# A fused AFNO / GEGLU kernel: the gate/up contraction recut into pairs of 192 columns, the weight chain reordered

## The chip, the core and the metric

The kernel runs on one core of a Trainium2 chip. The metric is device time in microseconds of one execution; the time before is the median of three runs. TensorE multiplies, VectorE and ScalarE read its results out of PSUM, GpSimd takes a part of the elementwise work, SyncE issues nearly all transfers.

## The reference

One sequence of 8192 tokens with 448 features is normalised per token; two branches read it. The first is a spectral one: a Fourier transform over the tokens, a two-layer complex MLP in four blocks of 112 with ReLU and soft threshold, and the inverse transform. The second is a GEGLU feed-forward with 1792 hidden features. The output joins them.

```python
xn = layernorm(x)                                     # [8192, 448]
s  = irfft(softshrink(mlp2(relu(mlp1(rfft(xn))))))    # along the 8192 tokens
g  = silu((gelu(xn @ w_gate) * (xn @ w_up)) @ w_down) # 448 -> 1792 -> 448
out = x + s * g
```

## The kernel before

All products are made from fp16 halves: a value is split into hi and lo, and hi·hi + hi·lo + lo·hi are summed in PSUM, three matmuls for each tile of 128 contraction rows. TensorE's stream is led by the feed-forward; all else is put between its matmuls.

The feed-forward goes over the 14 tiles of 128 hidden features in two passes (`PF`): pass 0 with 8 tiles, whose partial result goes to memory (`prt`), pass 1 with 6. Each pass goes over 16 chunks of 512 tokens. Chunks 0 and 1 of pass 0 are multiplied plainly (`plain()`); all others use a Winograd form with seven products in place of eight: the token pairs and the 448 contraction columns are halved, the latter into K1 = 256 and K2 = 192. A *unit* (`unit()`) is two hidden tiles of one chunk: its steps a1 to a7 call `product(k)` for the seven classes, for each of the two tiles. The operand combinations of the tokens are made by `factors()` in the first phase, written to memory (`xts`), and read back transposed, XA / 128 = 16 tiles of them as `xta` and 9 as `xtb`. The combinations of the weights are made by `gu_comb()`. A class whose two row tiles are full takes six matmuls for one hidden tile; one whose second tile holds 64 hi and 64 lo rows takes five:

```python
PROD = {1: (0, 4), 5: (4, 8), 6: (8, 10), 7: (12, 12), 2: (3, 6), 4: (6, 14), 3: (0, 2)}
if k in (1, 5, 6, 7):
    seq = [(s, v + j, xb + 2 * d + j) for j in range(2) for s, d in ((0, 0), (0, 1), (1, 0))]
else:
    seq = [(0, v, xb), (0, v, xb + 2), (1, v, xb), (0, v + 1, xb + 1), (1, v + 1, xb + 1)]
```

The order of steps in a unit of `chunk()` is: product 5, product 6, product 4 of the unit before, product 2, product 3, product 1 of the next unit, product 7. ScalarE copies product 5 out (`copy5`), and VectorE adds the bank of products 1 and 6 to it (`sum5`); products 3 and 7 wait for that sum.

The down product of a chunk follows its units. It is plain at first (`down()`: 8 tiles x 4 token tiles x 3 = 96 matmuls of 448 columns) and takes a seven-product form (`down2()`: 7 x 4 x 2 x 3 = 168 matmuls of 224 columns and one of 64) from the first chunk at whose start `state` has "products", that is, once `factor0()` has written the combined down weights; that form also needs sums of the hidden values (`sums()`) and, in the middle of the next chunk's first unit, its own tail.

The spectral branch has three phases around it. Phase 1 (`chunk1()`) normalises the tokens of a chunk, makes the factors and the first Fourier stage (`stage1()`, three matmuls for each token tile); phase 2 (`group()`, 64 of them) does the second stage and the MLP, with `zero()` for frequency 0; phase 3 (`tiles3()`) the last stage and the output. The weight chain (`weights()`) runs beside phase 1: `gu_split()` and `gu_comb()` of the 8 near tiles, `factor0()`, the 6 far tiles in pairs (`far_block()`), the far down weights (`down_weights(1)`), the MLP weights (`prep_mlp()`). Staging tiles come from rings: `WS` for gate/up weights (4 buffers in the prologue, then 1), `WD`, `CB`, `WO`.

The order of all instructions is fixed when the kernel is built: generators are run by a planner (`Pace`) that keeps a model clock for each engine and starts work at times set by constants (`STEPS`, `T1`, `DT`, `END1` to `END3`). `calm()` and `lull()` put an instruction off until the planner sees its engine free. Every engine then runs its own list in order, and waits on semaphores.

Of the kernel before, what the change touches and what calls it, by code (L numbers as in the profile page):

```python
# [36 lines left out]
XA, XW = 4 * 2 * K1, 4 * 2 * K1 + 3 * 2 * K2  # L37
SL = 11
# [3 lines left out]
STEPS = ((0, 2.75, 0.05, 0.97), (100, 2.5, 0.2, 1.03), (175, 3, 0.15, 1.0), (250, 2.75, 0.1, 1), (325, 2.5, 0.05, 1.01), (400, 2.75, 0.05, 1.04), (475, 3.0, 0.05, 1), (550, 3.5, 0.05, 1.01), (700, 2.75, 0.05, 1.02), (775, 2.0, 0.1, 0.985), (850, 2.25, 0.05, 0.97), (925, 2.75, 0.05, 1.04), (1150, 2.75, 0.05, 0.985), (1450, 2.5, 0.05, 1.01), (1525, 2.75, 0.15, 0.99))  # L42
# [342 lines left out]
def fft_constants():  # L385
# [45 lines left out]
    def triple(v, scale):  # L431
        hi, lo = _split(v * scale)
        return np.stack([hi, lo, (hi.astype(np.float64) * 2.0 ** -11).astype(np.float16)], axis=1)

    small = np.concatenate([
# [9 lines left out]
        "c_small": np.ascontiguousarray(small),  # L445
    }
# [3 lines left out]
def lay_out(a):  # L450

    up, gate = (np.asarray(a[k]).reshape(D, NF, 128) for k in ("B_w_up", "B_w_gate"))
    gu = np.zeros((NF, 128, SL, 128), np.float32)
    for s, w in ((0, up), (4, gate)):
        gu[:, :, s:s + 3] = w[:384].reshape(3, 128, NF, 128).transpose(2, 1, 0, 3)
    for s, w, r in ((3, up, 384), (7, gate, 384), (8, gate, 128), (10, up, 128)):
        gu[:, :64, s] = gu[:, 64:, s] = w[r:r + 64].transpose(1, 0, 2)
    gu[:, :64, 9] = gu[:, :64, 3]
# [5 lines left out]
        "in_gu": gu.reshape(NF, 128, SL * 128),  # L464
# [9 lines left out]
def afno_geglu_kernel(ctx, tc, x, gu, wd, mlp, b1, b2, c_m, c_mt, c_small, out):  # L474
# [44 lines left out]
    ident = cp.tile([128, 128], F16, name="ident")  # L519

# [4 lines left out]
    fm = cp.tile([128, 2, 2, NBK], F32, name="fm")  # L525
    fx = cp.tile([128, 2, 2 * NBK], F32, name="fx")
# [27 lines left out]
    def largest(dst, src, floor):  # L554
# [11 lines left out]
        V.tensor_scalar(dst, b[:, 128:128 + w], floor, None, op0=ALU.max)  # L566
# [20 lines left out]
    p1 = r1.enter_context(tc.tile_pool(name="p1", bufs=1, side="right"))  # L587
    X4 = ring(p1, [128, CH, D], F32, "x4", 2)
# [4 lines left out]
    SX = ring(p1, [128, 4 * 480], F16, "sx", 2)  # L593
    MX = ring(p1, [8, 1], BF16, "mxr", 2)
    identb = p1.tile([128, 128], BF16, name="identb")
# [3 lines left out]
    WS = ring(wp, [128, SL * 128], F32, "wst", 4)  # L599
# [197 lines left out]
    def far_block(b):  # L797
# [9 lines left out]
        for i in range(2):  # L807
# [5 lines left out]
            if i == 0:  # L813
                WS.put(t)
# [1867 lines left out]
```

## Time and profile before

| | |
|---|---|
| median of three runs | 1755.29 us (1753.55 to 1756.8) |
| profiled execution | 1756.02 us, span 1754.1 us |
| granted TensorE clock, mean | 0.997 |
| TensorE busy | 1724.0 us, 16218 matmuls |
| VectorE / ScalarE / GpSimd busy | 1432.7 / 1123.8 / 739.2 us |
| traffic | 304.16 MB, mean 173 GB/s |

A matmul's busy time overlaps that of its neighbours, so the time of one is read from the distance of two starts. A tile's name stands for all its buffers; nearly every instruction has the same line, since one helper issues them, and so groups are told apart by their tiles: `wt` are gate/up weights, `dw` down weights, `h` and `left` the hidden values, `xs` the token halves, `bx`, `by`, `bd` PSUM banks.

### The profile page before, as it was taken

How to read it: one execution, taken by the hardware profiler on the slowest of the kernel's cores; microseconds unless marked ns; L12 is line 12 of the kernel's file. 1: busy time of each engine (PE TensorE's matmuls, PEld its weight loads, DVE VectorE, ACT ScalarE, POOL GpSimd, SP SyncE). 2: the span in 40 equal slices, each digit the busy share in tenths (PEclk: the TensorE clock that was granted, in tenths of full speed). 3: DMA queues.
4: the chain of work that ended last, by engine and by line, in shares of the span. 5: the costliest groups of instructions: out<-in, count | busy, mean ns of one | idle time of the engine just before them, and what ended most of it. 6: DMA issues, size and time to landing. Idle time of an engine off the chain costs nothing.

```text
span 1754.1 us, 41652 instructions
## 1 busy us (share of the span) xinstructions
PE 1724.0 (98%) x16218; PEld 1489.0 (85%) x16218; DVE 1432.7 (82%) x2558; ACT 1123.8 (64%) x2244; POOL 739.2 (42%) x910
## 2 busy tenths in 40 slices
PE   8999999999999999999999999999999999999998
PEld 4447678899888899999989899898999889888887
DVE  7868677887988978777888787899888887788888
ACT  6557666666667666566887777777777775433334
POOL 2124333655666755253533545455434442122221
PEclk9999999999999999999999999999999999999999
DMA  6374788665666664323456755654456545999986
GB/s 224 104 214 151 202 229 220 192 192 167 166 202 208 197 169 126 73 63 93 107 164 189 177 122 130 153 129 103 122 137 144 129 103 132 300 293 330 312 249 223
DMA packets 402006, 304.16 MB, mean 173 GB/s; under 512 B 272688, under 2 KB 372912, under 8 KB 401808
## 3 DMA queue, kind: packets, MB, share of 16 engines
q1 hardware_dynamic: 401664, 301.46, 61.2%
q8 instruction: 127, 2.08, 0.5%
q14 instruction: 71, 0.58, 0.1%
q10 hardware_dynamic: 144, 0.03, 0.0%
HBM read 131.44 MB, written 106.15 MB: 135 GB/s over the span
## 4 chain that ended last, share of the span: by engine, by line
PE 82%; DVE 9%; ACT 3%; issue 2%; DMA 2%; SPq 1%; POOL 1%; DVEq 0%; ACTq 0%
PE bd L234 33%; PE bx L234 27%; PE by L234 22%; DVE h L234 2%; DVE wt L234 1%; ACT h L234 1%; SPq L234 1%; DVE u L234 1%; DVE left L234 1%; DVE va L234 1%; DVE v L234 0%; DMA vt<-va 0%; DMA wsp<-wo 0%; DVE by L234 0%; ACT wt L234 0%
## 5 line engine op out<-in xcount | busy, mean ns | idle before, releaser
L234 PEld LDWEIGHTS <-wt 128*128 128x128 f16 x9350 | 905.8, 98 | 168.8 <-issue 12.4
L234 PE MATMUL bx<-xta,wt 128*128 128x256 f16 (+1 forms) x2979 | 371.6, 275 | 3.2 <-DVE by L234 2.6
L234 PEld LDWEIGHTS <-h 128*128 128x128 f16 x2716 | 258.8, 98 | 36.4 <-DVE h L234 3.9
L234 PE MATMUL by<-xtb,wt 128*128 128x256 f16 x2080 | 256.4, 273 | 3.4 <-DVE by L234 3.4
L234 PE MATMUL bd<-dw,h 128*128 128x224 f16 (+1 forms) x1266 | 171.0, 280 | 1.2 <-DVE h L234 1.1
L234 POOL TENSOR_TENSOR wt<-wt 128x256 f32<-128x256 f32 x97 | 76.6, 790 | 200.1 <-DVE wt L234 182.4
L234 PE MATMUL by<-xta,wt 128*128 128x256 f16 (+1 forms) x1059 | 141.8, 281 | 3.2 <-ACT wt L234 3.1
L234 PE MATMUL bx<-xtb,wt 128*128 128x256 f16 x1040 | 131.6, 274 | 0.5 <-DVE v L234 0.4
L234 ACT ACTIVATE u<-by,fc 128x512 f32<-128x512 f32 (+1 forms) x118 | 73.6, 636 | 49.7 <-PE by L234 46.7
L234 PE MATMUL bx<-left,wt 128*128 128x256 f16 x864 | 105.1, 273 | 0.0
L234 DVE TENSOR_TENSOR by<-bx,u 128x512 f32<-128x512 f32 x104 | 72.1, 693 | 38.8 <-PE bx L234 32.4
L234 PE MATMUL bd<-dw,wt 128*128 128x224 f16 (+1 forms) x816 | 98.7, 264 | 2.2 <-DVE left L234 1.8
L234 ACT COPY u<-by 128x512 f32<-128x512 f32 x104 | 60.8, 585 | 61.5 <-PE by L234 61.2
L234 ACT CAST h<-wt 128x512 f16<-128x512 f32 (+1 forms) x128 | 68.5, 536 | 34.9 <-DVE wt L234 27.9
L234 PE MATMUL bd<-wt,h 128*128 128x224 f16 x693 | 84.3, 259 | 1.2 <-DVE h L234 1.1
L234 PEld LDWEIGHTS <-left 128*128 128x128 f16 x864 | 81.9, 98 | 3.1 <-issue 0.8
L234 DVE TENSOR_TENSOR v<-bx,u 128x512 f32<-128x512 f32 x104 | 71.2, 685 | 13.6 <-PE bx L234 12.6
L234 ACT COPY by<-bx 128x512 f32<-128x512 f32 x104 | 60.0, 577 | 34.8 <-PE bx L234 34.6
L234 PE MATMUL bd<-w2t,wn 113*128 113x112 f16 (+1 forms) x1152 | 77.3, 212 | 0.9 <-DVE bd L234 0.7
L234 DVE SCALAR_TENSOR_TENSOR left<-bd,ms,left 128x448 f32<-128x448 f32 x96 | 64.3, 677 | 16.9 <-PE bd L234 15.9
L234 ACT ACTIVATE th<-bd,ms 128x448 f32<-128x448 f32 x62 | 38.6, 634 | 59.6 <-PE bd L234 54.4
L234 POOL TENSOR_TENSOR t<-h 112x256 f32<-112x256 f32 (+1 forms) x40 | 35.1, 877 | 96.3 <-ACT h L234 73.9
(294 smaller groups left out, 3797.8 us busy)
## 6 DMA issues: line engine op xcount, KB each, us to landing
xts<-sx SPq DMA_DIRECT2D x32, 480.0 KB, 2.9
x<-in_x SPq DMA_DIRECT2D x17, 896.0 KB, 6.4
t<-ysb SPq DMA_DIRECT2D x64, 224.0 KB, 3.2
prt<-th SPq DMA_DIRECT2D x64, 224.0 KB, 2.7
vt<-va SPq DMA_DIRECT2D x256, 56.0 KB, 2.1
left<-prt SPq DMA_DIRECT2D x64, 224.0 KB, 3.7
u<-t SPq DMA_DIRECT2D x32, 448.0 KB, 5.8
x<-in_x SPq DMA_DIRECT2D x32, 448.0 KB, 6.3
```

The source lines that it names most:

```text
L234: return self.pace.issue(self.name, kind, out, ins, lambda: fn(out, *args, **kw))
```

## The change

The contraction is cut anew. The halves are 192 pairs of columns, of the 64 left over 63 are dealt to three product classes of 21 each (`KP`), and column 255 is folded in by subtracting a token's sum, which the normalisation on ScalarE now accumulates. Classes 1, 4 and 7 now have two full tiles, classes 2, 3, 5 and 6 a mixed second one; `xtb` has 11 tiles. `factors()` is written anew: it casts 832 columns and subtracts 1664 in each half chunk (before 1024 and 1856), has seven small GpSimd operations, and writes seven pieces in place of five. `gu_comb()` makes all of `wt[..][2:16]` from a weight layout of 17 tiles (`raw`), and holds its staging buffer to the end.

The weight chain: `WS` has 3 buffers in the prologue, `CB` and `WD` are gone; the maxima of the far weights are taken by a chain of their own (`maxima()`), each far tile is then loaded once (`far_tile()`), `factor0()` runs on one staging buffer, and `prep_mlp()` has no pauses. The second `plain` chunk's down product now comes before three quarters of the first's. The seven-product down form starts at chunk 9 of pass 0 at the earliest. The planner's constants are set anew (`DT` 34.5, `END2` 1450, `END3` 1730). The bf16 identity is read from the fp16 one's bits, the mask of the two row kinds (`c_rows`) is loaded in the prologue.

```diff
-WS = ring(wp, [128, SL * 128], F32, "wst", 4)
-CB = ring(wp, [128, 8, 128], F32, "cb", 1)
+WS = ring(wp, [128, SL * 128], F32, "wst", 3)
...
     def norm_act(c, a):
-        S.activation(x4[:, a, :], x4[:, a, :], AF.Identity, bias=st[:, a, 8:9], scale=st[:, a, 11:12])
+        S.activation(x4[:, a, :], x4[:, a, :], AF.Identity, bias=st[:, a, 8:9], scale=st[:, a, 11:12],
+                     accum_out=st[:, a, 0:1])
...
     def factors(c, q, xs):
+        S.copy(v[:, 0, 0:K1], sf[:, 3, :])
+        S.copy(v[:, 1:4, 0:K2], sf[:, 0:3, 0:K2])
+        yield from B.calm("tensor_sub", v[:, 0, K1:], sf[:, 3, :], v[:, 0, 0:K1])
+        yield from B.calm("tensor_sub", v[:, 1:4, K1:K1 + 128], sf[:, 0:3, 0:128], v[:, 1:4, 0:128])
+        yield from B.calm("tensor_sub", v[:, 1:4, K2:K1], sf[:, 0:3, 128:K2], v[:, 1:4, 128:K2])
...
+        G.tensor_copy(v[:, 1:3, 384:448], v[:, 1:3, 128:K2])
+        G.tensor_copy(v[:, 1:4, 448:448 + 2 * KP].rearrange("p i (s k) -> p i s k", k=KP),
+                      h.rearrange("p s (i k) -> p i s k", k=KP))
+        G.tensor_copy(v[:, 1:4, 448 + 2 * KP:448 + 3 * KP], h[:, 0].rearrange("p (i k) -> p i k", k=KP))
+        G.tensor_scalar(v[:, 1:4, 511], st[:, 0].to_broadcast([128, 3]), -1.0, None, op0=ALU.mult)
...
+        G.tensor_copy(w[:, :, 0:KP], v[:, 0].rearrange("p (s c) -> p s c", s=2)[:, :, K2:K2 + KP])
+        G.tensor_copy(w[:, :, KP:3 * KP], xs[:, 1, :, K2 + KP:K2 + 3 * KP])
+        G.tensor_scalar(w[:, :, 63], st[:, 1].to_broadcast([128, 2]), -0.5, None, op0=ALU.mult)
...
-    T1, DT = 85.0, 37.0
+    T1, DT = 85.0, 34.5
...
     def gu_combs(fs):
+            if f == 2:
+                yield ev("dw", 7)
-            e = pace.spawn(gu_comb(f, EV["wst", f, 1], wt[f][:, :, 8:16]))
+            e = pace.spawn(gu_comb(f, EV["wst", f, 1], wt[f][:, :, 2:16]))
...
-    PROD = {1: (0, 4), 5: (4, 8), 6: (8, 10), 7: (12, 12), 2: (3, 6), 4: (6, 14), 3: (0, 2)}
+    PROD = {1: (0, 4), 7: (4, 12), 5: (8, 8), 6: (12, 10), 2: (3, 6), 4: (7, 14), 3: (0, 2)}
...
-            if k in (1, 5, 6, 7):
+            if k in (1, 4, 7):
                 seq = [(s, v + j, xb + 2 * d + j) for j in range(2) for s, d in ((0, 0), (0, 1), (1, 0))]
             else:
-                seq = [(0, v, xb), (0, v, xb + 2), (1, v, xb), (0, v + 1, xb + 1), (1, v + 1, xb + 1)]
+                seq = [(0, v, xb), (0, v, xb + 2), (1, v, xb), (0, v + 1, xb + 1),
+                       (1, v + 1, xb + (1 if k == 3 else 3))]
...
     def ffn():
-        for a in range(CH):
-            yield from down(0, 0, a, 0, nf, EV["hT", 0])
-            yield pe()
-        HT.put(h)
+        yield from down(0, 0, 0, 0, nf, EV["hT", 0])
+        yield pe()
         ...
+        for a in range(1, CH):
+            yield from down(0, 0, a, 0, nf, EV["hT", 0])
+            yield pe()
+        HT.put(h)
...
     def chunk(p, i):
-        if "products" in state and "seven" not in state:
+        if "products" in state and "seven" not in state and (p or i >= 9):
...
-    END1, END2, END3 = T1 + NG * DT + 12.0, 1438.0, 1732.0
+    END1, END2, END3 = T1 + NG * DT + 12.0, 1450.0, 1730.0
...
     def weights():
         room()
+        most = pace.spawn(maxima())
         for e in [pace.spawn(factor0(j)) for j in range(PF[0][1] // 2)]:
             yield e
-        for b in range(*PB[1]):
-            yield pace.spawn(far_block(b))
+        for f in range(PF[1][0], NF):
+            yield from far_tile(f)
+        yield most
```

## Rows read from the trace of the kernel before

**Rows 1.** The page: engines' busy time; shares of the chain that ended last.

```profile
PE 1724.0 (98%) x16218; PEld 1489.0 (85%) x16218; DVE 1432.7 (82%) x2558; ACT 1123.8 (64%) x2244; POOL 739.2 (42%) x910
...
PE 82%; DVE 9%; ACT 3%; issue 2%; DMA 2%; SPq 1%; POOL 1%; DVEq 0%; ACTq 0%
```

**Rows 2.** Table by stretch: length, busy us of each engine, granted clock, DMA.

```profile
200.00:300.00 100.00, 95.35 (x766) 74.61 (x765) 68.27 (x126) 59.64 (x112) 31.46 (x48) 1.00 0.75 220
300.00:400.00 100.00, 100.00 (x932) 89.89 (x931) 86.32 (x147) 69.46 (x135) 59.24 (x79) 1.00 0.69 198
600.00:700.00 100.00, 99.51 (x947) 91.41 (x945) 84.32 (x169) 64.55 (x125) 58.73 (x74) 1.00 0.57 161
950.00:1488.00 538.00, 529.38 (x5598) 485.08 (x5596) 448.66 (x776) 390.93 (x816) 245.30 (x273) 1.00 0.54 132
985.00:990.00 5.00, 5.00 (x31) 4.15 (x30) 2.69 (x5) 2.90 (x7) 0.75 (x2) 0.66 0.74 223
```

**Rows 3.** Timeline of TensorE: start, us, instruction; two gate/up groups.

```profile
338.29 1.47 PE L234 MATMUL bx<-xta,wt 128*128 128x256 f16 x12
339.60 1.26 PE L234 MATMUL bx<-xtb,wt 128*128 128x256 f16 x10
```

**Rows 4.** Timeline of TensorE: plain down product, then the seven-product form.

```profile
245.61 9.81 PE L234 MATMUL bd<-dw,h 128*128 128x448 f16 x51
255.26 0.73 PE L234 MATMUL bd<-xs,m 128*128 128x448 f16 x3
...
300.78 1.31 PE L234 MATMUL bd<-dw,h 128*128 128x224 f16 x12
301.93 1.92 PE L234 MATMUL by<-dw,h 128*128 128x224 f16 x19
```

**Rows 5.** Tile u: ns min/median/max, first and last start us, shapes.

```profile
L234 DVE TENSOR_TENSOR by<-bx,u x104: 679/698/700, 153.6 to 1726.4; 128x512 f32<-128x512 f32 x104
...
L234 DVE TENSOR_TENSOR h<-u,h x49: 676/691/2129, 28.9 to 934.9; 128x512 f16<-128x512 f32 x49
```

**Rows 6.** Tile left: fetch of the seven-product form's factors.

```profile
L234 SPq DMA_DIRECT2D left<-dsp x8: 429/430/441, 279.3 to 282.6; - x8
```

**Rows 7.** TensorE's groups by form: count | busy us, mean ns | idle.

```profile
L234 PE MATMUL bd<-dw,h 128*128 128x448 f16 x288 | 56.8, 352 | 0.0
...
L234 PE MATMUL bd<-xs,m 128*128 128x448 f16 x174 | 42.2, 352 | 0.0
```

**Rows 8.** Timeline of TensorE: products behind the VectorE sum, holes in brackets.

```profile
154.32 1.25 PE L234 MATMUL by<-xtb,wt 128*128 128x256 f16 x10 [1.00 <-DVE by L234]
...
210.90 1.25 PE L234 MATMUL by<-xtb,wt 128*128 128x256 f16 x10 [1.93 <-DVE by L234]
...
267.03 2.35 PE L234 MATMUL by<-xtb,wt 128*128 128x256 f16 x20
...
296.46 1.47 PE L234 MATMUL bx<-xta,wt 128*128 128x256 f16 x12 [2.62 <-DVE by L234]
```

**Rows 9.** Timeline of SyncE: loads of gate/up weights in the prologue.

```profile
26.05 0.34 SPq L234 DMA_DIRECT2D wst<-in_gu  x1
...
32.91 14.93 SPq L234 DMA_DIRECT2D wst<-in_gu  x4
```

**Rows 10.** Timeline of TensorE, prologue: two waits for scaled weights.

```profile
41.45 1.68 PE L234 MATMUL by<-xta,wt 128*128 128x512 f16 x7 [1.39 <-ACT wt L234]
...
58.45 1.47 PE L234 MATMUL by<-xta,wt 128*128 128x512 f16 x6 [1.69 <-ACT wt L234]
```

**Rows 11.** GpSimd's groups by form, 85 to 700 us: small operations.

```profile
L234 POOL TENSOR_TENSOR sx<-sf,sx 128x64 f16<-128x64 f32 x24 | 13.7, 571 | 14.3 <-ACT sx L234 14.3
...
L234 POOL TENSOR_SCALAR st<-st 128x4 f32<-128x4 f32 x32 | 9.6, 299 | 42.6 <-DVE st L234 41.0
```

**Rows 12.** Tile wn: the memset that opens the second phase.

```profile
L234 POOL MEMSET wn<- x2: 1376/1376/1377, 733.3 to 734.6; 128x1536 f16 x2
```

**Rows 13.** TensorE's waits: releaser, total us, times, longest.

```profile
PE bd L234 <- DMA vt<-va: 2.9, 1, 2.9
```

More of the change, by code (lines that the diff above doesn't have):

```diff
@@ new lines, in maxima @@
+    def maxima():
+        for b in range(*PB[1]):
+            for k in range(2):
+                for i in range(2):
+                    yield from maximum(fm[:, k, i:i + 1, b], 512, raw[BLK[b][0] + k].rearrange(
+                        "p (s c) -> p s c", c=128)[:, 10 * i:10 * i + 7:2])
+            mx = fx[:, :, b]
+            V.tensor_tensor(mx, fm[:, 0, :, b], fm[:, 1, :, b], op=ALU.max)
+            yield
+            yield from largest(fx[:, :, NBK + b], upper(fx)[:, :, b], 2.0 ** -30)
+            scales(b)
+            yield
+            scales_of_products(b)
+            done("scales", b)
+        for f in range(PF[1][0], NF):
+            yield from maximum(dmx[:, f:f + 1], D, wd[128 * f:128 * f + 128, :])
@@ L833, in far_block @@
-        e = pace.spawn(work(f0 + 1, t))
-        t = yield from load(f0)
-        yield e
-        yield from work(f0, t)
+        Q.dma_start(wsp[f - PF[1][0]], d.rearrange("p s v c -> p (s v c)"))
+        WO.put(d)
     def gu_block(b):
@@ L938, in gu_comb @@
         yield from calm("DVE")
-        V.scalar_tensor_tensor(d[:, 1], c, scale(f, 0), d[:, 0], op0=ALU.mult, op1=ALU.subtract)
-        R.put(cb)
+        V.scalar_tensor_tensor(t[:, 11], t[:, 2], keep_a, t[:, 12], op0=ALU.mult, op1=ALU.add)
+        if far:
+            tasks.append(pace.spawn(first()))
+        yield from sub(t[0:64, 3], t[0:64, 6], t[0:64, 3])
+        yield from B.calm("tensor_add", t[0:64, 7], t[0:64, 7], t[0:64, 2])
+        yield
+        yield from sub(t[:, 2], t[:, 4], t[:, 0])
@@ new lines, in gu_comb @@
+        if far:
+            tasks.append(pace.spawn(second()))
+        done("taken", f)
+        yield
+        yield from sub(t[:, 5], t[:, 14], t[:, 2])
+        if not far:
+            yield ev("spare", f - 2 if f < 6 else f) if f >= 2 else ev("hp", 1, f)
+            tasks = [pace.spawn(g) for g in (first(), second(), halves(slice(10, 12), slice(8, 10)))]
+        tasks.append(pace.spawn(halves(slice(12, 14), slice(5, 8, 2))))
+        for e in tasks:
+            yield e
+        WS.put(ws)
@@ L1035, in split @@
             rings[f].put(t)
-        for e in [pace.spawn(most(*q)) for q in parts]:
+        for e in [pace.spawn(most(*q)) for q in parts] if p == 0 else []:
             yield e
@@ L1081, in room @@
     def room():
-        nonlocal WS, CB, WO, WD
+        nonlocal WS, WO, WM
         rw.close()
```

356 lines of the change are left out of this document (188 added, 168 removed).

## The prediction

> **What bounds the kernel now.** I read the page first. TensorE is busy for 1724.0 of 1754.1 us and 82% of the chain that ended last lies on it [rows 1]: the span is the length of one in-order matmul stream plus its holes, 30.1 us in all. The table by stretch says where the holes are: none from 300 to 400 us, 0.5 in 600 to 700, 4.65 in 200 to 300 and 8.6 from 950 to 1488 [rows 2]; the rest lies in the prologue and at the end, where the last results drain. VectorE is at 84 to 86% in the first pass but off the chain. So I price an edit first in columns that TensorE no longer streams or streams anew, and then in holes.
>
> The timeline gives the price of a column. Twelve gate/up matmuls of 256 columns begin at 338.29, the next group at 339.60: 1.31/12 = 0.1092 us each [rows 3]. In the plain down product 51 matmuls of 448 columns take 255.26 - 245.61 = 9.65 us, 0.1892 us each; in the seven-product form twelve of 224 columns take 301.93 - 300.78 = 1.15 us, 0.0958 each [rows 4].
>
> **The change, part by part.**
>
> *The recut.* A unit (two weight tiles, one chunk) runs seven products for each of its two tiles. Now four of the classes take six matmuls and three take five, 39 for a tile; after it three take six and four take five, 38. That is two fewer in each unit. Units are counted by the one sum that each needs, by<-bx,u: 104 [rows 5]. 208 x 0.1092 = **-22.7 us**, all on the stream that sets the end. Nothing excludes this term: the sequences stand in product().
>
> *The guard on chunk 9.* Now the seven-product down form begins as soon as its factors are ready: they are fetched by 279.3 [rows 6], and there are 288 plain matmuls of 448 columns on h, that is three chunks of 96: chunk 0, 2 and 3 [rows 7] (chunk 1's read another tile). So it begins with chunk 4. The new condition lets it begin with chunk 9 at the earliest. Chunks 4 to 8 turn plain: each streams 96 x 0.1892 = 18.2 us instead of 168 x 0.0958 + 0.03 = 16.1 us, +2.04 us. Five chunks: **+10.2 us**. The reordered chain fetches the factors of the first pass one after another through one staging buffer; even at twice the present length it would be ready before chunk 9, which began near 533 us in the old pace, so I count five and not more.
>
> *Holes at the head of a plain chunk.* There the order is product 1, 5, 6, 2, 3, and product 3 waits for the VectorE sum of products 5 and 6. Only product 2 (10 matmuls, 1.09 us) covers that sum, which alone takes 0.70 us [rows 5]; any operation ahead of it on VectorE shows. In a seven-product chunk the previous chunk's tail stands there and hides it. The trace has three heads behind a plain chunk: holes of 1.00 and 1.93 us, and none at the third, at 267 us; mean 0.98 [rows 8]. Five more: **+4.9 us**, between 0 and 9.7 (all at 1.93). I take the mean because the five come in the stretch of rows 2 where VectorE is busiest, and because what they shed (the operand sums of the seven-product form) is about what the denser first phase adds.
>
> *Three staging buffers instead of four in the first pass.* The load of the sixth weight tile goes out at 26.05, when the second tile's buffer is free; the next one at 32.91, when the third's is [rows 9]. With three buffers the sixth tile takes that later place, 6.9 us later. TensorE waits 1.39 us at 41.45 for the weights that are scaled with it, then 1.69 us at 58.45 for the next pair [rows 10]. Bounds: nothing (another chunk's matmuls fill the hole) and +6.9. I take **+2.5 us**, under the middle: the second wait then has later work in front and may go.
>
> *Vector work.* The new factors() casts 832 columns instead of 1024 and subtracts 1664 instead of 1856 in each half chunk, but adds two accumulator reads on ScalarE and seven GpSimd operations, 224 in all. The nearest rows, small GpSimd operations, mean 299 and 571 ns [rows 11]: 67 to 128 us more on GpSimd, which is idle 41% of 600 to 700 us [rows 2]. The heavier gu_comb lies in a chain that TensorE reads only when the tile's next user comes; its new waits (the last down weight, the chunk-1 down product) only place it later in the order of ScalarE and VectorE. SyncE issues seven stores instead of five in each half chunk, 64 more, and a longer second transpose; queued behind them are token loads and the next chunk's transposes, which have a whole down product, 18 us, before they are read. Cost **0**; if the vector cover is gone it is the fourth rival.
>
> *The order of the two plain chunks, the bf16 identity, the mask's load on ScalarE's queue, the layer-1 order, the add behind the memset on GpSimd:* the same matmuls in another order, and issues while ScalarE waits for the first tokens, **0**; the chunk-1 down product now frees the weight tiles some 13 us earlier than chunk 2 needs them, and the hole in front of chunk 2 is already under 0.2 us.
>
> *prep_mlp without its pauses:* small VectorE operations now come in runs, and a waiting sum can stand behind one. Between 0 and 2.6 us, the longest such hole [rows 8]; I take **+0.5**, what that stretch now idles [rows 2].
>
> *The second phase.* It starts at 733.3 [rows 12], when the first phase and the MLP weights behind it are done. The planner's step of phase 1 falls from 37 to 34.5 us: 16 x 2.5 = 40 us earlier. Its end mark moves 12 us later, so the 64 groups get some 797 instead of 745 us. The holes there are 8.6 us [rows 2], 2.9 of them one wait for a transfer [rows 13], behind which the granted clock of 985 to 990 us is 0.66 on average, between its levels of 2.4 and 1.2 GHz [rows 2]: 0.34 x 5 = 1.7 us more. Between 0 and -10.3; I take a quarter, **-2.5**, for the 7% lower density and the chance that this one wait does not recur.
>
> Sum: -22.7 + 10.2 + 4.9 + 2.5 + 0.5 - 2.5 = -7.1 us. The profiled execution took 1756.0 us (span 1754.1 and 1.9 around it), so 1748.9; it stands 0.7 above the median of the three runs, so as a median **1748 us**.
>
> **Where a rule of the skill speaks against it.** Two VectorE rows show GpSimd's hand: the sum by<-bx,u, with one operand in PSUM, never takes over 700 ns; h<-u,h, of the same size with both operands in SBUF, has median 691 and maximum 2129 [rows 5]. The Trainium skill, "SBUF — State Buffer", section "Who interferes with whom", says that a VectorE instruction with two SBUF inputs and a GpSimd instruction that reads SBUF take one shared port as an exclusive lock, the loser waiting for the whole instruction. By that rule the 224 new GpSimd operations lengthen VectorE's chain too, which is the fourth rival. The trace agrees as far as the two rows go.
>
> **The rivals.**
>
> 1. *The plain chunks cost no hole, and the second phase relaxes.* For it: the third head had no hole, and VectorE sheds the operand sums in five chunks. Against: the first two. -22.7 + 10.2, then up to -6 of the second phase's holes: -12.5 to -18.5, about 1740 us.
>
> 2. *The gain is eaten at the heads and in the prologue.* All five heads at the longest hole behind that sum, 2.62 us [rows 8]: +13.1; prologue +4; no relief. -22.7 + 10.2 + 13.1 + 4 + 0.5 = +5.1 at worst, -3 at best: 1752 to 1761, no change to be measured. For it: the weight chain, which stood before sums at the first two heads, runs at all five now.
>
> 3. *The seven-product form starts even later than chunk 9,* because the factor chain stalls on its one buffer: each further chunk costs 2.04 + 0.98 = 3.0 us, so two would halve the gain (1754). Against it: 370 us of slack as counted above. I give it no case of its own; it is in the second's chance.
>
> 4. *Slower: phase 1's vector chain becomes the bound.* The 58 stage-1 triples (174 matmuls [rows 7]) stand in TensorE's queue at planned times and each waits for a low half from VectorE or GpSimd; all gate/up matmuls queue behind. Today none waits [rows 2]. If the denser phase 1 and the GpSimd operations make each wait one small GpSimd operation, 0.30 to 0.57 us, that is +17 to +33 us: 1766 to 1782. It cancels the gain from 7.1/58 = 0.12 us a triple. For it: VectorE at 86% there, the long maxima of h<-u,h. Against: five plain chunks are lighter just there.
>
> **How the numbers follow.** About 0.2% (3.5 us) is what a measurement of this kernel can tell from no change. My forecast, -13 to -3, has 0.52; the first rival 0.20; the second 0.17; the fourth 0.11. Faster by over 0.2%: nearly all of the first two, 0.70. Within it: most of the second rival and the edge of the forecast, 0.15. Slower: the fourth and the worse end of the second, 0.15. The range goes from 1738 (recut and guard alone with most of the relief) to 1760 (second rival's worse end); beyond lie the fourth rival and the far end of the first, some 0.15 to 0.2.
>
> **What would show it.** Matmuls: 16218 - 208 - 5 x 73 = 15645, and 768 plain ones of 448 columns on h instead of 288. No product on left before some 570 us. Groups of ten in products 5 and 6 at the same 0.109 us. Holes at the heads of chunks 3 to 9 in the chain of waits, from VectorE's sum. First second-phase memset near 690 us. The prediction is wrong in its main step if the unit's matmuls do not fall by two or the spacing of a matmul grows; wrong in size if the holes from 262 to 540 us are far from 5 us; wrong in sign if stage-1 matmuls wait on xs.

## The result: slower by a third of a per cent, and the profile after

The changed kernel takes 1760.29 us (median of 20 runs, 1755.88 to 1764.61), the kernel before beside it 1754.39 (20 runs, 1752.17 to 1758.08); the ratio is 1.0033, 95% interval 1.0025 to 1.0041. The forecast was 1748, faster. The profiled execution after took 1758.21 us, span 1756.4: 2.3 us more span than before, and 2.1 us under its own median, where the profiled execution before stood 1.6 above its own. So of the 5.9 us between the medians the two profiles hold only 2.2; the other 3.7 are in neither trace.

The page after: busy time and count of each engine [rows 1].

```profile
PE 1715.7 (98%) x15645; PEld 1435.9 (82%) x15645; DVE 1418.7 (81%) x2606; ACT 1113.9 (63%) x2279; POOL 751.5 (43%) x1083
```

TensorE's groups by form: the plain down product on `h` [rows 7].

```profile
L235 PE MATMUL bd<-dw,h 128*128 128x448 f16 x768 | 152.4, 353 | 0.0
```

The counts are those forecast, 15645 matmuls and 768 plain ones. The stream became shorter as computed; 40.7 us of the span are now idle (1756.4 - 1715.7) where 30.1 were, and the 1715.7 busy us hold more half clock than before. The table by stretch after (length, then busy us of TensorE, of its weight loads, of VectorE, ScalarE and GpSimd, then granted clock, busy share of the DMA engines and GB/s) shows where [rows 2]; idle is the length less TensorE's busy time:

```profile
0.00:20.00 20.00, 16.02 (x82) 8.16 (x82) 12.19 (x26) 9.38 (x20) 5.19 (x19) 0.83 0.70 239
20.00:50.00 30.00, 27.23 (x139) 13.20 (x139) 22.82 (x44) 21.13 (x55) 6.51 (x12) 0.94 0.54 177
50.00:85.00 35.00, 31.72 (x149) 14.11 (x148) 32.07 (x63) 21.26 (x42) 10.56 (x14) 0.95 0.41 136
85.00:120.00 35.00, 34.18 (x163) 15.57 (x161) 33.09 (x67) 23.32 (x41) 21.05 (x29) 1.00 0.29 107
120.00:160.00 40.00, 37.54 (x201) 20.18 (x199) 34.74 (x73) 27.74 (x57) 32.12 (x55) 0.96 0.78 232
160.00:200.00 40.00, 37.59 (x314) 30.50 (x313) 35.30 (x69) 30.50 (x63) 26.39 (x46) 1.00 0.75 231
200.00:300.00 100.00, 99.39 (x750) 72.74 (x749) 79.28 (x150) 68.17 (x135) 63.48 (x117) 1.00 0.92 272
300.00:500.00 200.00, 199.52 (x1490) 145.16 (x1488) 148.75 (x285) 132.72 (x261) 115.67 (x222) 1.00 0.78 224
500.00:700.00 200.00, 198.18 (x1827) 173.31 (x1825) 155.40 (x319) 126.43 (x262) 110.36 (x175) 1.00 0.60 160
1700.00:1770.00 70.00, 45.12 (x399) 38.16 (x397) 44.19 (x72) 19.26 (x34) 12.89 (x13) 0.94 0.59 207
```

Two rows of the same table before:

```profile
20.00:85.00 65.00, 61.46 (x312) 28.55 (x312) 55.07 (x119) 44.88 (x101) 10.82 (x16) 1.00 0.44 143
1700.00:1755.00 55.00, 48.47 (x445) 42.76 (x443) 43.29 (x74) 20.39 (x36) 10.81 (x12) 0.98 0.61 211
```

Before, 20 to 200 us idled 4.5 us in all (3.5 up to 85 us, 1.0 behind), at full clock; now 11.7 (6.1 and 5.7), with three drops of the clock. From 200 to 500 us before idled 4.65, now 1.1. Behind 1700 us the span idled 5.6 before (1754.1 - 1700 - 48.5), now 11.3 (1756.4 - 1700 - 45.1).

The timeline of TensorE after, holes in brackets, in the prologue and at chunk 2 [rows 8, 10]:

```profile
41.96 2.10 PE L235 MATMUL by<-xta,wt 128*128 128x512 f16 x7 [1.45 <-ACT wt L235]
57.95 0.17 PE L235 MATMUL bd<-ident,mxr 2*128 2x2 bf16 x1 [1.47 <-DVE mxr L235]
...
155.81 2.71 PE L235 MATMUL bx<-xta,wt 128*128 128x256 f16 x12 [2.46 <-DMA xta<-xts]
171.78 1.47 PE L235 MATMUL bx<-xtb,wt 128*128 128x256 f16 x12 [1.24 <-DVE v L235]
```

Chunk 2's first product begins at 155.81 (before: 147.56) and waits for its tiles. The timeline of SyncE after: that load is issued at 148.49 (before: 119.79), behind chunk 2's last store (141.75) and five stores of chunk 3.

```profile
141.75 0.39 SPq L235 DMA_DIRECT2D xts<-sx  x1
144.41 3.98 SPq L235 DMA_DIRECT2D xts<-xs  x5
148.49 4.36 SPq L235 DMA_TRANSPOSE xta<-xts  x1
```

Three windows after show the clock: 0.52, 0.53 and 0.76 on average, between the levels of 2.4 and 1.2 GHz.

```profile
43.00:46.00 3.00, 3.00 (x11) 1.23 (x10) 3.00 (x5) 2.38 (x7) 1.15 (x1) 0.52 0.00 0
60.00:63.00 3.00, 2.53 (x10) 1.03 (x10) 2.96 (x4) 2.94 (x8) 1.45 (x2) 0.53 0.00 0
153.00:160.00 7.00, 4.54 (x26) 3.16 (x25) 6.83 (x13) 3.59 (x7) 4.92 (x11) 0.76 1.02 219
```

With some 3.4 us at the lower level each costs about 1.7 us. The end of the timeline of TensorE after:

```profile
1742.76 2.46 PE L235 MATMUL bd<-u,mt 128*128 128x448 f16 x18 [0.96 <-DMA mt<-c_mt]
1746.49 0.45 PE L235 MATMUL bx<-wt,h 128*128 128x224 f16 x3
```

The last group of matmuls starts at 1746.49 (before: 1748.02), 1.5 us sooner where 12.5 had been counted; and 9.5 us of last results follow it, where before had 5.6.

**The ledger.** Span after less span before, from the two profiled executions, each idle term from the stretches, beside the prediction's term. The columns are counted, at the prediction's prices; e2 and e3 below measure them.

| term | predicted | measured, us |
|---|---|---|
| columns: recut and guard | -12.5 | -12.5 |
| 0 to 20 us, idle | 0 | -0.5 |
| 20 to 200 us, idle | +2.5 | +7.2 |
| 20 to 200 us, three drops of the clock | 0 | +5.1 |
| 200 to 500 us, the heads | +4.9 | -3.6 |
| 500 to 700 us, `prep_mlp` | +0.5 | +0.8 |
| 700 to 1500 us, idle +0.4, one drop fewer -1.7 | -2.5 | -1.3 |
| 1500 to 1700 us, idle | 0 | +0.6 |
| behind 1700 us | 0 | +5.7 |
| sum | -7.1 | +1.5 (span: +2.3) |

The 0.8 left over is busy time that no row here places.

### The profile page after: what moved, and what is told of

Read it like the earlier page. It is cut to its first block, busy times and chain, and to the rows that moved or that the text cites. A ratio compares the mean times of both kernels' runs of the same rounds, so it can differ in the third digit from the quotient of the medians.

```text
span 1756.4 us, 40962 instructions
## 1 busy us (share of the span) xinstructions
PE 1715.7 (98%) x15645; PEld 1435.9 (82%) x15645; DVE 1418.7 (81%) x2606; ACT 1113.9 (63%) x2279; POOL 751.5 (43%) x1083
## 4 chain that ended last, share of the span: by engine, by line
PE 84%; DVE 7%; DMA 3%; ACT 3%; issue 2%; SPq 1%; POOL 1%; DVEq 0%; ACTq 0%; POOLq 0%
PE bd L235 34%; PE bx L235 29%; PE by L235 21%; DVE wt L235 1%; DVE u L235 1%; SPq L235 1%; DVE h L235 1%; DMA wst<-in_gu 1%; DMA prt<-th 1%; DVE va L235 1%; DMA xtb<-xts 1%; ACT h L235 1%; DVE o L235 0%; DMA vt<-va 0%; ACT o L235 0%
## 5 line engine op out<-in xcount | busy, mean ns | idle before, releaser
L235 PEld LDWEIGHTS <-wt 128*128 128x128 f16 x9142 | 887.2, 98 | 173.8 <-issue 19.4
L235 PE MATMUL bx<-xta,wt 128*128 128x256 f16 (+1 forms) x2819 | 355.5, 276 | 3.5 <-DMA xta<-xts 2.5
L235 PE MATMUL bd<-dw,h 128*128 128x448 f16 (+1 forms) x1536 | 243.2, 306 | 0.0
L235 PE MATMUL bx<-xtb,wt 128*128 128x256 f16 x1248 | 153.2, 273 | 2.4 <-DVE v L235 2.3
L235 POOL TENSOR_TENSOR wt<-wt 128x256 f32<-128x256 f32 x81 | 63.0, 778 | 209.8 <-DVE wt L235 198.7
L235 PE MATMUL by<-xta,wt 128*128 128x256 f16 (+1 forms) x899 | 126.4, 285 | 2.7 <-ACT wt L235 1.9
L235 DVE TENSOR_TENSOR v<-bx,u 128x512 f32<-128x512 f32 x104 | 71.1, 684 | 16.1 <-PE bx L235 15.2
L235 POOL TENSOR_TENSOR t<-h 112x256 f32<-112x256 f32 (+1 forms) x36 | 30.0, 832 | 114.3 <-ACT h L235 93.1
L235 PE MATMUL bd<-wt,h 128*128 128x224 f16 x603 | 72.2, 259 | 0.8 <-DVE h L235 0.7
L235 DVE SCALAR_TENSOR_TENSOR u<-by,fc,u 128x512 f32<-128x512 f32 (+1 forms) x86 | 55.4, 658 | 21.5 <-PE by L235 11.9
L235 PEld LDWEIGHTS <-wn 113*128 113x128 f16 (+1 forms) x1152 | 69.1, 97 | 3.8 <-POOL wn L235 0.6
```

What stands on the lines that cost most here:

```text
L235: return self.pace.issue(self.name, kind, out, ins, lambda: fn(out, *args, **kw))
```

## The experiments

Each row of the table is one kernel: its median and its ratio to the kernel before on the same chip, and from its own profile the idle time of TensorE by stretch. "Extra" is busy time beyond the columns at full clock: 1722.3 us for before's stream (1724.0 less the 1.7 of its one drop), 1709.8 after recut and guard, and so on by the prediction's terms. (The order of some puts twenty-four matmuls of 224 columns for twelve of 448 in the third phase; that costs nothing.) Most of the extra time is half clock, but not all: by an estimate from the granted clock over TensorE's busy time, 4.9 of 5.9 us after, 12.6 of 18.4 in e1 and 3.4 of 6.4 in e12. A profile is one execution, and some stand off their median: e7's is 5.8 us above it, e9's 5.3, e6's 3.4.

```
kernel                     median   ratio [95%]              extra  idle  20-200  200-1700  >1700
before                     1754.39  1                          1.7  30.1     4.5      15.5    5.6
after                      1760.29  1.0033 [1.0025,1.0041]     5.9  40.7    11.7      13.7   11.3
e1  after, no guard        1793.64  1.0234 [1.0220,1.0248]    18.4  72.8    12.2      37.4   19.1
e2  before + guard         1764.62  1.0063 [1.0051,1.0076]     1.8  28.5     4.5      13.0    7.0
e3  after + 208 matmuls    1782.46  1.0164 [1.0149,1.0179]     8.1  40.2    12.8      15.3    6.8
e4  after, shared buffers  1772.01  1.0105 [1.0091,1.0119]     9.5  52.8    10.9      30.5    7.0
e5  after, stores later    1760.81  1.0042 [1.0029,1.0054]     9.0  41.9    12.0      15.2   10.9
e6  after, ends 1438/1715  1756.39  1.0013 [1.0004,1.0022]     7.2  41.0    14.7      14.7    6.9
e7  after, T1 78           1763.48  1.0051 [1.0037,1.0065]    12.9  44.1    10.5      22.5    6.8
e8  after, thin weights    1782.62  1.0160 [1.0144,1.0175]    15.3  55.7     8.8      35.8    6.8
e9  after, old plan        1768.44  1.0080 [1.0061,1.0098]    14.1  47.9     8.1      29.9    6.2
e10 no guard, old plan     1766.93  1.0076 [1.0061,1.0092]    12.8  52.0     9.0      32.5    6.5
e11 before, new plan       1778.88  1.0142 [1.0126,1.0157]     4.0  49.7     1.4      23.9   19.9
e12 before, T1 78          1768.65  1.0083 [1.0069,1.0097]     6.4  40.6     4.7      23.5    7.0
e13 after, ends 1430/1715  1760.76  1.0039 [1.0026,1.0052]     8.2  41.0    13.0      17.3    6.9
e14 after, ends 1438/1700  1757.37  1.0015 [1.0007,1.0024]     7.1  38.2    13.0      13.8    6.8
e15 e6, seven from chunk 8 1765.67  1.0064 [1.0049,1.0079]    13.4  45.8    12.2      22.4    7.3
e16 before, ends 1450/1730 1766.46  1.0067 [1.0054,1.0080]     4.5  37.9     4.6      13.8   15.2
e17 e6, T1 81              1768.67  1.0080 [1.0066,1.0093]     8.5  49.9    11.1      26.7    6.9
e18 e6, T1 91              1767.38  1.0071 [1.0057,1.0085]    10.1  46.9    11.0      24.4    7.3
```

**e1, the guard taken out.**

```diff
-        if "products" in state and "seven" not in state and (p or i >= 9):
+        if "products" in state and "seven" not in state:
```

> The changed kernel with the seven-matmul down product allowed from chunk 4 on, as in the kernel before, instead of from chunk 9; all else as changed. Against the changed kernel at 1760.3 us: the prediction's term for the guard (10.2 us) and its holes at the heads of five plain chunks (4.9) make it 15 us faster, 1745. My reading of the trace after (the heads show 0.48 us of idle time from 300 to 500 us, so there is nothing there to win) makes it 10 us faster, 1750. A rival, that the guard is there because the left products' vector work slows the first phase by as much as the matmuls save, makes it 1758 to 1762.

Measured: 1793.64, 33 us slower instead of 10 to 15 faster. Three windows of its table by stretch:

```profile
300.00:500.00 200.00, 191.07 (x1769) 171.62 (x1768) 168.30 (x303) 129.65 (x268) 133.36 (x227) 0.99 0.72 199
900.00:1200.00 300.00, 286.84 (x3010) 260.90 (x3008) 244.29 (x422) 207.88 (x436) 127.99 (x146) 0.99 0.58 149
1700.00:1800.00 100.00, 71.66 (x623) 61.08 (x620) 64.51 (x104) 27.91 (x49) 20.30 (x21) 0.90 0.62 206
```

The stream is 10.2 us shorter by the term, 288 plain matmuls as before. The loss is spread: 8.9 us idle from 300 to 500, 13.2 from 900 to 1200, 19.1 behind 1700, and 18.4 us of extra busy time in all, some 12.6 of it half clock. None of the three theories had this.

**e2, the guard alone, on the kernel before** (the same line, the other way).

> The kernel before with nothing changed but the guard: the seven-matmul form from chunk 9 on instead of chunk 4. Against the kernel before at 1754.4 us: by the prediction +10.2 for five chunks and +4.9 for the holes at their heads, 1769.5; without holes 1764.6; under 1757 if the plain chunks free vector work that the first phase was short of.

Measured: 1764.62 against 1754.13 beside it, +10.5. The page's line of engines:

```profile
PE 1734.3 (98%) x15865; PEld 1457.0 (83%) x15865; DVE 1383.6 (78%) x2509; ACT 1103.2 (63%) x2183; POOL 646.7 (37%) x805
```

TensorE's busy time rose by 10.3 us (1734.3 - 1724.0). From 200 to 500 us it idles 1.2 us where before had 4.65 [rows 2]: the plain heads cost next to no hole. VectorE is relieved by 49 us (1432.7 to 1383.6). A hole of 4.71 us at 573.54, which the kernel before doesn't have, takes back what the heads save. So the guard's term holds as a price in columns, and the term for the heads does not; that the median too moved by just 10.5 is partly luck.

**e3, one matmul more in each tile.**

```diff
+                seq += seq[-1:] if k == 5 else []
```

> The changed kernel with the last matmul of product class 5 issued twice in each gate/up tile (39 instead of 38 a tile, 208 more in all, so one term of that class is counted twice). If the first phase runs at TensorE's pace, 208 x 0.1092 us = 22.7 us more, 1783. If the recut's gain was not realised because another engine set the pace of the gate/up stretches, the added matmuls fall into idle time and it costs under 10 us, 1760 to 1770.

Measured: 1782.46, 22.2 us more than the changed kernel.

```profile
PE 1740.6 (98%) x15865; PEld 1458.6 (82%) x15865; DVE 1436.1 (81%) x2641; ACT 1114.6 (63%) x2272; POOL 715.1 (40%) x1055
```

TensorE's busy time rose by 24.9 us (1740.6 - 1715.7), 22.7 by the count and 2.2 extra. TensorE's stream sets the pace of the gate/up stretches; the recut's 22.7 us are real.

**e4, two weight tiles in one staging buffer.**

```diff
-            t = yield from WS.get()
+            if again or f % 2 == 0:
+                t = yield from WS.get()
...
+            k = 0 if again else f % 2 * 8 * 128
...
-            Q.dma_start(t[:, 0:n], (raw if again else gu)[f])
+            Q.dma_start(t[:, k:k + n], (raw if again else gu)[f])
...
-            WS.put(t)
+            if i == n - 1:
+                WS.put(t)
```

> The changed kernel, but the two weight tiles of a pair in the prologue's first pass share the two halves of one staging buffer, so that six tiles can be on their way in the three buffers instead of three. If the weight loads waiting for a buffer are what made the prologue late (first down product 5.8 us later than before), the reduce at 37.8 us no longer waits 1.8 us for its load, the holes from 39 to 68 us shrink, and it is 3 to 6 us faster, 1754 to 1757. If the prologue is bound by the vector work of the combined and the remade weights, under 1 us, 1759.5 to 1760.5.

The wait went: VectorE's group of maxima from 20 to 85 us, changed kernel and e4, the last column the idle time ahead and what ended it.

```profile
L235 DVE TENSOR_REDUCE fm<-wst 128x2 f32<-128x1024 f32 x6 | 7.1, 1212 | 1.8 <-DMA wst<-in_gu 1.8
```

```profile
L235 DVE TENSOR_REDUCE fm<-wst 128x2 f32<-128x1024 f32 x6 | 7.1, 1211 | 0.0
```

From 20 to 85 us the idle time fell from 6.1 to 3.9: 2.1 us, near the 2.5 that the prediction gave the buffers; and the clock of that stretch is 1.00 where it was 0.95 after: the two drops, another 3.4 us, are gone too. Yet the time rose by 12: from 200 to 1700 us it idles 30.5 instead of 13.7. No instruction was added; the sooner release of a buffer gave the build's planner another order, which idles more.

**e5, chunk 3's stores held back.**

```diff
+            if c == PL + 1:
+                yield ev("xt", "a", 0, PL)
```

> The changed kernel with chunk 3's five stores held back until the transposing load of chunk 2's tiles has been issued. If those stores, standing ahead of that load on SP's queue, are why chunk 2's gate/up waits 2.46 us at 155.8 us, the wait goes and with it the 3 us of half clock behind it: 2.5 to 4.2 us faster, 1756 to 1758. If the load is late because chunk 2's own stores end late (142 us), at most 1 us.

Measured: 1760.81, no gain. The timeline of TensorE in e5:

```profile
155.53 1.47 PE L235 MATMUL bx<-xta,wt 128*128 128x256 f16 x12 [1.62 <-DMA xta<-xts]
164.03 2.29 PE L235 MATMUL by<-xtb,wt 128*128 128x256 f16 x10 [3.19 <-DVE by L235]
```

The wait for the tiles only shrank from 2.46 to 1.62 us, and a product behind it waits 3.19 for VectorE's sum. SyncE's timeline in e5 shows that the five stores were not the cause:

```profile
142.44 0.39 SPq L235 DMA_DIRECT2D xts<-sx  x1
148.60 4.07 SPq L235 DMA_TRANSPOSE xta<-xts  x1
```

With nothing between, the load still goes out at 148.60, when chunk 2's last store, issued at 142.44, has landed: SyncE waits 5.7 us there for it. So the stores come too late. In part they land slowly. The transfers of that time after, from 128 to 149 us, and before, from 105 to 120 (KB each, then us from issue to landing):

```profile
wst<-in_raw SPq DMA_DIRECT2D x3, 1088.0 KB, 8.2
xts<-sx SPq DMA_DIRECT2D x2, 480.0 KB, 7.7
```

```profile
xts<-sx SPq DMA_DIRECT2D x2, 480.0 KB, 2.7
```

The same stores that landed in 2.7 us before take 7.7, beside three weight loads of 1088 KB that the remaking of the weights asks for; that these loads are the cause is argued, no run held them back. But most of the delay is older. The last subtraction that writes `sx` of chunk 2 ends at 135.70 (before: 113.36), 22.3 us later; the small GpSimd operations that are new in `factors()` then end at 140.83, another 5.1; and from there to the load it takes 7.7 us, where before took 6.4. That makes the 28.7 us by which the load is late (148.49 - 119.79).

**e6, e13, e14, the end marks of the second and third phase.**

```diff
-    END1, END2, END3 = T1 + NG * DT + 12.0, 1450.0, 1730.0
+    END1, END2, END3 = T1 + NG * DT + 12.0, 1438.0, 1715.0
```

> The changed kernel with the ends of its second and third phase that the pacing aims at set from 1450 and 1730 to 1438 and 1715 us. If the work of the last phase comes too late because it is paced for a stream that ends at 1730, the 9.5 us behind the last matmul shrink towards the 5.6 of the kernel before: 3 to 5 us faster, 1755 to 1757. If the tail hangs on something else, within 1 us of 1760.3.

> The changed kernel with the end marks of the second and third phase at 1430 and 1715 us (1450 and 1730 as changed; 1438 and 1715 gave 1756.4). If the third phase's length of plan is what empties the tail, it stays near 6.9 us behind 1700 and the time is 1753 to 1757; if a second phase pressed by 20 us waits for its transfers, 1758 to 1765.

> The changed kernel with the end marks at 1438 and 1700 us. If 6.9 us behind 1700 is the floor of the tail (last products, their transfers), no gain over 1756.4; if the third phase's work is still planned too late, 2 us more, 1754.

Measured: 1756.39, 1760.76 and 1757.37. The tail falls to 6.9, 6.9 and 6.8 us in all three, and e6 is 3.9 us faster than the changed kernel (3.5 by the ratios to the kernel before beside each). A mark of 1700 brings no more (its 1.0 us lies within the intervals); at 1430 the stretch from 1200 to 1500 idles 8.1 us (3.7 after). e6 is the best version of the changed kernel that was found, and it is still behind the kernel before by 1.0013 (1.0004 to 1.0022).

**e16, those marks alone on the kernel before** (1450 and 1730 for 1438 and 1732).

> The kernel before with only the changed kernel's end marks, 1450 and 1730 instead of 1438 and 1732. If the third phase, planned into 280 us instead of 294, comes too late and drains behind the stream, the idle time behind 1700 us rises from 5.6 to 10 or more and it is 3 to 8 us slower, 1757 to 1762. If the longer tail of the changed kernel comes of its other work, within 1 us of 1754.

Measured: 1766.46 against 1754.52, +12. It idles as the kernel before in every stretch up to 900 us (4.62 from 200 to 300, 0.00 from 300 to 500, 1.07 and 0.21 behind), and behind 1700 us 15.2 instead of 5.6. The timeline of TensorE and the last stretch:

```profile
1746.27 3.54 PE L234 MATMUL bd<-u,mt 128*128 128x448 f16 x9 [4.57 <-DMA mt<-c_mt]
```

```profile
1700.00:1770.00 70.00, 49.52 (x418) 40.73 (x415) 46.08 (x77) 19.76 (x35) 11.20 (x12) 0.88 0.56 197
```

TensorE waits 4.57 us for a load of the third phase. SyncE issued the last three of these at 1735.84, 1738.31 and 1744.59 us; in the kernel before the last went out at 1728.00. From 1744 to 1752 us the granted clock is 0.59. The added tail is the marks' own.

**e7, the first phase planned to start at 78 instead of 85 us** (`T1`).

> The changed kernel with the planned start of the first phase's deferred work, 85 us, set to 78 us. If the vector work between the prologue and chunk 2 is planned too late, the chunk's tiles are ready sooner and it gains 1 to 3 us, 1757 to 1759. If it is only a plan and the work is late for want of engine time, nothing or a loss up to 3 us, 1760 to 1763.

Measured: 1763.48, +3. Chunk 2's tiles are loaded 11 us sooner, at 137.46, and yet from 20 to 200 us 10.5 us are idle. Later it has one hole of 9.31 us; the timelines of VectorE, GpSimd and TensorE there, one fence each:

```profile
577.25 0.43 DVE L235 TENSOR_TENSOR u<-gl,u 128x256 f32<-128x256 f32 x1 [10.02 <-POOL gl L235]
579.01 0.68 DVE L235 TENSOR_TENSOR v<-bx,u 128x512 f32<-128x512 f32 x1
```

```profile
575.63 0.10 POOL L235 MEMSET mst<- 128x4 f32 x1 [20.77 <-DMA dsp<-wo]
575.70 0.72 POOL L235 TENSOR_TENSOR gl<-gl 128x256 f32<-128x256 f32 x1
```

```profile
579.74 2.50 PE L235 MATMUL bx<-xtb,wt 128*128 128x256 f16 x11 [9.31 <-DVE v L235]
```

GpSimd's queue holds a 0.10 us memset of `prep_mlp`; it waits 20.77 us, at last for a store of down factors, which SyncE issues at 570.84 behind a row of 26 loads. Behind it stands GpSimd's half of a hidden sum, behind that VectorE's next sum, behind that TensorE. In the changed kernel the same memset stands elsewhere (523.9), and there is no such hole. One small instruction in another place of one in-order queue cost four tenths of what the recut gives.

**e8, the near tiles' weights not recombined.** In the changed `gu_comb()`, with `mix()` in place of `sub()` at seven places, and one addition left out in the same way:

```diff
+        def mix(o, p, q):
+            if far:
+                yield from sub(o, p, q)
...
-        yield from sub(t[:, 0:4], t[:, 0:4], t[:, 10:14])
+        yield from mix(t[:, 0:4], t[:, 0:4], t[:, 10:14])
```

> The changed kernel with the nine additions and subtractions that recombine a remade gate/up tile left out for the eight near tiles (the weights of those tiles are then not the products' weights; the far tiles are unchanged). They are most of the tile's VectorE and GpSimd work on wst, 53 instructions and 34 us of the two engines from 85 to 200 us. If that work is what makes the stretch from 50 to 200 us late, idle time there falls from 9.0 us to about before's 2.7 and the kernel gains 5 to 8 us, 1752 to 1755. If TensorE there waits for the fetch of chunk 2's tiles and the first tiles' scaled weights, under 2 us, 1758.5 to 1760.5.

Eight additions and subtractions a tile are left out, not nine. From 20 to 200 us the idle time falls by 3.0 us, from 11.7 to 8.8, not to before's 4.5. At chunk 2 the forecast came: the load of its tiles goes out at 132.43 instead of 148.49, nothing waits for them, and 150 to 200 us idles 1.5 us instead of 4.9 (before 1.0). Against it stands a new hole of 2.64 us at 94.26. And since e9, with all its weight work, has 8.1 in all and 3.1 from 150 to 200, a part of this is order; the run doesn't settle the share of the recombination. The time is 22 us worse, with 35.8 us idle from 200 to 1700.

**e9 to e11, the planner's constants exchanged.** `STEPS`, `DT` and the end marks of the kernel before in the changed kernel (e9), in e1 (e10), and the changed kernel's in the kernel before (e11).

> The changed kernel with the constants by which the build orders the work (the table of steps, 37 us for a chunk, 1438 and 1732 for the ends) set as they were before the change. If the loss is in the work itself, the constants matter little: 1757 to 1763. If the constants were what paid for the change, or the order they give is decisive, it moves by over 5 us either way.

> The changed kernel without the guard and with the ordering constants of before. Without the guard it took 1793.6 with the new constants. If those 33 us come of constants that fit a plain first phase, they vanish here: 1750 to 1760. If they come of the seven-matmul form's vector work on top of the recut's (VectorE 1485 us busy against 1419), it stays at 1780 to 1800.

> The kernel before with the changed kernel's ordering constants and nothing else. If the order matters little, 1752 to 1757. If each set of constants fits one kernel alone, 5 to 40 us slower, with the added holes spread over the whole span, as without the guard.

Measured: 1768.44, 1766.93 and 1778.88. The constants are worth 8 us to the changed kernel, 27 us the other way to e1 and 25 us to the kernel before. With the old constants the guard costs 1.5 us (1768.44 - 1766.93), which is within the intervals, where its columns cost 10.2 and where, with the new ones, it gains 33.

**e12, one constant alone, on the kernel before** (`T1` 78 instead of 85).

> The kernel before with one constant of the ordering changed: the planned start of the first phase's chunks 78 us instead of 85. No instruction is added or taken away, only placed differently. If the kernel before stands at an order that was fitted, and any other order is worse, it is 5 to 25 us slower with more idle time and more half clock on TensorE, 1760 to 1780. If its low idle time is a property of its work, it stays within 3 us, 1751 to 1757.

Measured: 1768.65, +14, without one instruction of the change. Three rows of its table by stretch:

```profile
500.00:700.00 200.00, 196.71 (x1842) 177.76 (x1839) 177.90 (x325) 129.62 (x250) 120.48 (x150) 1.00 0.58 161
1200.00:1500.00 300.00, 293.72 (x3085) 269.39 (x3084) 248.82 (x428) 205.37 (x433) 146.41 (x155) 1.00 0.52 127
1500.00:1700.00 200.00, 196.17 (x1782) 173.44 (x1781) 158.45 (x259) 71.84 (x125) 44.53 (x46) 0.99 1.00 304
```

The idle time of 200 to 1700 us rose from 15.5 to 23.5, in small pieces, and the extra busy time from 1.7 to 6.4 us. The low idle time of the kernel before is a property of its order.

**e15, e17, e18, three more orders of e6:** the seven-product form from chunk 8 on, `T1` 81, `T1` 91.

> The changed kernel with the end marks 1438 and 1715 and the seven-matmul form from chunk 8 on instead of 9. By the prediction's term one chunk fewer in the plain form saves 2.0 us of stream: 1754.4 against 1756.4. If every change of the order costs its fit, it is 3 to 20 us slower, 1759 to 1776, by idle time and clock, with the stream 2 us shorter as counted.

> The changed kernel with end marks 1438 and 1715 and the planned start of the first phase 81 us instead of 85. Any other order costs its fit: 1757 to 1775 where 1756.4 was had at 85. A version under 1753 would show that a better fit of the changed kernel is near.

> As the one before, with the planned start at 91 us: 1757 to 1775 if any other order costs its fit; under 1753 if a first phase planned 6 us later, as the prologue really runs 5.8 us later, fits better.

Measured: 1765.67, 1768.67 and 1767.38, all 9 to 12 us slower than e6. In e15 the stream is 2.0 us shorter by the term and the time 9.3 us longer. In e17 one hole at 579.86 us, of 11.25 us, is the one of e7.

## Why the prediction was wrong

**The recut, -22.7, was right,** by the count and by e3 (22.2 for the same number of matmuls). **The guard, +10.2, was right** as a price in columns, by e2 (10.5).

**The heads, +4.9, were the wrong way.** They cost next to nothing in e2 and in the changed kernel (1.2 and 1.1 us idle from 200 to 500 us); the mean of three heads next to the prologue was taken for five that came later. The first rival had that part.

**Three staging buffers, +2.5, was right in idle time:** from 20 to 85 us 6.1 us are idle where 3.5 were, and e4 takes 2.1 back. The two drops of the clock there, 3.4 us, had no term.

**The step that failed is the one on the vector work and the two plain chunks:** "cost 0", since the chain is read only when the tile's next user comes, the transposes have a whole down product as cover, and the weight tiles are free 13 us sooner than needed. The next user, chunk 2, comes while the near tiles are still being remade. The table by stretch from 85 to 200 us, before and after:

```profile
85.00:200.00 115.00, 114.00 (x720) 70.26 (x718) 88.26 (x175) 72.44 (x121) 37.82 (x55) 1.00 0.63 183
```

```profile
85.00:200.00 115.00, 109.31 (x674) 66.25 (x672) 103.13 (x207) 81.57 (x160) 79.57 (x129) 0.99 0.62 194
```

The idle time there rose from 1.0 to 5.7 us, and one drop of the clock adds 1.7: 6.4 us where the prediction had nothing. VectorE's and GpSimd's busy time there (third and fifth) rose by 15 and 42 us. Chunk 2's token halves and their small GpSimd operations stand in these two queues among the weights, so the last store of `sx` goes out 27 us later (141.75, before 114.67), then lands slowly (e5), and its first sums stand behind the weights too. GpSimd's idle share, by which its operations were priced at nothing, says nothing of that: chunk 2's tiles wait for the last of them. How the loss divides between the remade weights and the new `factors()` is open. That some such loss belongs to the change's work is shown only by how every order fared: seven profiled orders of other constants or ends (e6, e7, e9, e13, e14, e17, e18) idle 8.1 to 14.7 us from 20 to 200 us, five orders of the kernel before (itself, e2, e11, e12, e16) 1.4 to 4.7.

**The second phase, -2.5, was read from one side.** "Its end mark moves 12 us later" was counted as relief. The third phase loses what the second gets: 1730 - 1450 = 280 us instead of 1732 - 1438 = 294, its last load of `mt` goes out at 1737.30 (before: 1728.00), and 5.7 us are lost behind 1700. e6 takes 3.9 us of the median back by the marks alone, and e16 shows 12 on the kernel before. Of the relief 1.3 us came, though the second phase's first memset comes at 647.9, not near 690 as forecast, so with more time still than was counted.

**The second rival was nearest** in its price (up to +5.1) and half in its mechanism: the prologue, but not the heads. That its price fits is luck: its 13.1 us at the heads did not come, the stretch to 200 us lost 12.3 instead of 4, and the tail's 5.7 stand in no rival. **The fourth rival did not come as a wait:** no stage-1 matmul waited. Tile u, then tile xs, after (ns min/median/max) [rows 5]:

```profile
L235 DVE TENSOR_TENSOR by<-bx,u x104: 679/699/700, 162.6 to 1720.5; 128x512 f32<-128x512 f32 x104
L235 DVE TENSOR_TENSOR h<-u,h x52: 673/682/1646, 28.6 to 955.6; 128x512 f16<-128x512 f32 x52
```

```profile
L235 PE MATMUL bd<-xs,m x174: 352/352/353, 21.5 to 578.1; 128*128 128x448 f16 x174
```

None of the 174 matmuls on `xs` is among TensorE's waits, and over the whole run these two sums of VectorE are as long as they were. GpSimd's whole load rose by only 12 us, since the guard took away what the recut added; against e2, with the same guard, it rose by 105 us (646.7 to 751.5), within the 67 to 128 that the prediction gave. The Trainium skill, "SBUF — State Buffer", section "Who interferes with whom", would have VectorE's sums with two SBUF operands lengthened by it. The row of h<-u,h, median 682 ns against 691 before, longest 1646 against 2129, does not show that; the stretch where the loss lies does. VectorE's groups from 85 to 150 us, one with both operands in SBUF and one with an operand in PSUM (the bank `by`), before and after (count | busy us, mean ns | idle):

```profile
L234 DVE TENSOR_TENSOR wst<-wst 128x128 f32<-128x128 f32 x5 | 1.7, 333 | 0.0
L234 DVE SCALAR_TENSOR_TENSOR u<-by,fc,u 128x512 f32<-128x512 f32 x6 | 4.5, 742 | 1.7 <-ACT u L234 1.7
```

```profile
L235 DVE TENSOR_TENSOR wst<-wst 128x128 f32<-128x128 f32 x9 | 4.4, 489 | 0.6 <-POOL wst L235 0.6
L235 DVE SCALAR_TENSOR_TENSOR u<-by,fc,u 128x512 f32<-128x512 f32 x7 | 5.2, 742 | 0.0
```

By an estimate from all two-input instructions of VectorE in that stretch whose inputs lie in SBUF, each less the shortest of its form in its trace, those that run beside a GpSimd instruction take 0.15 us more than that, the others 0.02, in both kernels; beside one run 67 of them after and 24 before. So some 6 of VectorE's added microseconds there are of the fourth rival's kind; what they cost TensorE is not shown.

**What lies beneath all terms:** each was priced with the rest of the order held. It is not held: the build's planner decides anew behind every edit. The change also sets the table `STEPS` anew, and no term of the prediction is for that. Nine kernels move constants alone (e7, e9, e11 to e14, e16 to e18), and they lie 1 to 25 us above the best known order of their program (the kernel before itself; e6), only e14 within the noise of it. An edit forecast at 7 us is smaller than that scatter. The recut's gain is there in columns in every profile; it is given back in idle time and half clock.

**What stays open:** whether an order of the changed kernel exists that idles as little as the kernel before does. The columns would then give 12.5 us, less what the prologue and chunk 2 keep: 12.3 as after, half clock included, or less. e6, e14, e17 and e18 looked close by and did not find it. Why e1 loses 33 us with the new constants and not with the old was not traced further than its spread over the whole span.

## What to carry to other kernels

In a kernel whose instruction order is built by a planner, price an edit twice: in the bound engine's columns, where the count held within half a microsecond here (10.5 for 10.2 in e2, 22.2 for 22.7 in e3), and in the fit of the order. Measure that fit before the edit, by moving one planning constant that changes no work; an edit smaller than the scatter can't be forecast without the new order itself. A deadline that is moved to relieve one stage is taken from the next. An engine's idle share does not make work on it free when a tile that the bound engine needs waits for the last of that work. And "read only later" is cover only if the reader's start is looked up against the whole queue that now stands ahead of it.

## What the runs showed of the hardware that was not expected

A hole does not always bring the lower clock. In the changed kernel the hole of 2.46 us at 155.81 is followed by some 3.4 us at 1.2 GHz; in e6, where the same product waits 2.78 us at 155.71, the same stretch holds full clock:

```profile
153.00:160.00 7.00, 4.29 (x40) 3.85 (x40) 6.83 (x13) 4.36 (x10) 4.92 (x10) 1.00 1.03 227
```

Four executions with the same order up to some 650 us (the changed kernel, e6, e13, e14) idle 5.7, 8.9, 7.0 and 7.2 us from 85 to 200 us, with one drop of the clock or none there: the same instructions in the same order scatter by 3 us in that stretch. The changed kernel's 20 runs spread over 8.7 us, the kernel before's over 5.9.
